# Attention and feed-forward on one core: three groups of tiles that TensorE reads, moved to other places modulo 512 bytes

## The chip, the core and the metric

The kernel runs on one core of one Trainium2 chip. The metric is the device time of one execution in microseconds; the time before is the median of three runs, 1213.74 us (1213.39 to 1214.49).

## What is computed

A layer norm feeds two branches, full attention with 32 heads of 16 and a feed-forward network with squared ReLU; their product, with a SiLU on the second, is added to the input. Cut to what matters:

```python
x = A_x                                   # 1 x 2048 x 512
xn = layernorm(x)
q, k, v = split_heads(xn @ A_wqkv)        # 32 heads of 16
p = softmax(q @ k.T * 16 ** -0.5)         # 32 x 2048 x 2048
s = merge_heads(p @ v) @ A_wo
h = relu(xn @ B_w1 + B_b1) ** 2           # 512 -> 1792
g = silu(h @ B_w2 + B_b2)                 # 1792 -> 512
return x + s * g
```

## The kernel before

Everything is float32. Matrix products other than that of the values are made in the faster float32r form from two parts of each operand, a high and a low one (h and l in the names of tiles), as high x high + high x low + low x high.

The kernel first normalizes and transposes the input and makes queries, keys and values with full-width matmuls (L127 in `linear`, L314 in `product`), and stores them in DRAM. Then the main loop goes over 64 turns of 8 steps. A step is four heads, 512 queries and 128 keys. In a turn TensorE does three things:

- Scores (L503): for each step four matmuls of 64 rows, weights 128 columns of the key tile KA, moving 512 columns of the query tile QA. Two of them, one in rows 0 to 63 and one in rows 64 to 127 of the array, run side by side. ScalarE takes the exponential of most (L507); some go through VectorE first (L526).
- Linear layers (L551, in `Block.issue`): the feed-forward network, later the output projection, in pieces between the scores, again two matmuls side by side in the two halves of the rows. First layer: weights wf1, moving the transposed input xh and xl. Second layer: weights the hidden values hh and hl, moving wf2. Output projection: weights the normalized attention output in reused tiles, moving wo in xh and xl.
- Values (L850): 8 steps of four matmuls of 32 columns each, weights slices of V (row kb of 83 numbers, 17 further for each head), moving the exponentials in P0 to P15. The profile lists each as two.

The order in a turn is written out as a string, such as `SLLSBLLLSLL0SL1LSLL/SBLLSLL0SL1LSLL0L1SLS`: S is two score matmuls, L one linear matmul in each half of the rows, 0, 1 and B are scores that go through VectorE, and / is the swap, at which the two halves change their bank and TensorE waits for a note by GpSimd (L577). VectorE and GpSimd split weights and hidden values into parts (L116, L120). SyncE loads QA, KA, V, weights and, a few turns ahead, the next xh and xl.

All tiles of SBUF are opened once at the start, by a table of names and sizes in `fast_path` (L103 to L110). Their order in it sets their addresses: a tile of n numbers takes 4n bytes of each partition, rounded up to 32, right behind the one before. P0 begins at a multiple of 512 bytes. Tiles of 1024 or 2048 numbers keep what is behind them at the same place modulo 512; a V tile of 16 x 83 = 1328 numbers takes 5312 bytes, 192 more than a multiple of 512; and each of the small tiles (st, rs, mv, okm, warm, ones, seen) takes 32 or 64. Matmuls address pieces of their tiles at distances that are multiples of 512 bytes, but for the values' slices of V.

Of the kernel before, what the change touches and what calls it, by code (L numbers as in the profile page):

```python
# [38 lines left out]
NK = S // 128  # L39
VW = 560  # L40
QW = 83
# [6 lines left out]
@with_exitstack  # L48
def mha_ffn_kernel(ctx: ExitStack, tc: tile.TileContext, x, wqkv, wo, bx, w1, b1, w2, b2, out):
    nc = tc.nc  # L50
    x, out = x[0], out[0]
    ctx.enter_context(tc.manual_schedule())
    keep = ctx.enter_context(tc.tile_pool(name="keep", bufs=1))
    dram = ctx.enter_context(tc.tile_pool(name="dram", bufs=1, space=DRAM))

    nvalid = keep.tile([1, 1], I32, name="nvalid")
    stat = keep.tile([128, 80], FT, name="stat")
    eps = keep.tile([128, 1], FT, name="eps")
    ident = keep.tile([128, 128], FT, name="ident")
    make_identity(nc, ident)  # L60

    kdram = [[dram.tile([128, 2, 1024], FT, name=f"kd{g}_{h}") for h in range(2)] for g in range(4)]
    qdram = [[dram.tile([128, 2, 512], FT, name=f"qd{g}_{c}") for c in range(NC)] for g in range(4)]
    vdram = dram.tile([NK, 128, VW], FT, name="vd")
    xdram = [dram.tile([128, 2, 4, 512], FT, name=f"xd{c}") for c in range(3)]
    sdram = {(a, p): dram.tile([128, 2, 4, 2, 128], FT, name=f"sd{a}{p}") for a in "kq" for p in range(2)}

    udram = [[dram.tile([2, 2, 16, 4, 512], FT, name=f"ud{g}_{c}") for c in range(NC)] for g in range(4)]
    zdram = [[dram.tile([4, 512], FT, name=f"zd{q}_{c}") for c in range(NC)] for q in range(NQ)]
    gdram = dram.tile([S, D], FT, name="gd")  # L70

    with tc.tile_pool(name="sb", bufs=1) as sb, ExitStack() as banks:
        fast_path(tc, sb, banks, locals())
    general_path(tc, dram, nvalid, ident, vdram, kdram, qdram, gdram, x, wo, out)


def fast_path(tc, sb, banks, env):
# [14 lines left out]
    def t(shape, dt, tag):  # L92

        cnt[0] += 1
        if tag in BUFS:
            turn[tag] = turn.get(tag, -1) + 1
            n = turn[tag] % BUFS[tag]
            p, tag = ps.get(tag), f"{tag}{places[n] if tag == 'S' else n}"
        else:
            p = None  # L100
        return (p or ps.get(tag, sb)).tile(shape, dt, tag=tag, name=f"{tag}_{cnt[0]}")

    split_tiles = [f"{a}{n}" for a in ("xh", "xl", "wf2h", "wf2l", "hh", "hl") for n in range(2)]  # L103
    for tags, n in (((f"P{i}" for i in range(16)), 1024), (("KA0", "KA1", "KA2"), 2048),
                    (("QA0", "QA1", "wf1h0", "wf1l0", *split_tiles), 1024),
                    (("T0", "T1", "wr0", "wr1", "gl", "u0", "u1", "y0", "y1"), 1024), (("ou0", "ou1", "b2b"), 512),
                    (("note",), 128), (("V0",), NK * QW), (("st0", "st1"), 12), (("rs0", "rs1", "mv0", "mv1"), 8),
                    (("okm", "warm"), 1), (("V1",), NK * QW)):
        for tag in tags:
            sb.tile([128, n], FT, tag=tag, name=f"{tag}_first")  # L110

# [451 lines left out]
    note, notes = t([1, 128], FT, "note"), [0]  # L563
# [264 lines left out]
    tags = (("P2", "gl", "P1"), ("P3", "P6", "P7"), ("wf2h0", "wf2l0", "wf2h1"), ("wf2l1", "gl", "KA2"))  # L828
# [196 lines left out]
    for j, c in enumerate(ORDER):  # L1025
        for i in range(2):
            n = per * (j + 1) + i - 1 if j < 3 else LAST + 2 + i
# [68 lines left out]
    seen = t([1, 16], FT, "seen")  # L1096
# [16 lines left out]
    for n in range(TURNS):  # L1113
        i = 8 * n
# [68 lines left out]
    ok, okm, ones = t([128, 80], FT, "ok"), t([128, 1], FT, "okm"), t([128, 1], FT, "ones")  # L1183
# [162 lines left out]
```

## Time and profile before

| | |
|---|---|
| Median of the runs | 1213.74 us |
| The profiled execution | 1212.94 us, of which the span from the first to the last instruction is 1211.2 |
| TensorE busy | 1200.1 us (99%) |
| ScalarE, VectorE, GpSimd busy | 1040.8 (86%), 845.4 (70%), 350.1 (29%) |
| Share of the DMA engines' time by the queue that SyncE feeds | 37.3% |
| Granted TensorE clock | 0.998 |

Lines of the profile name an engine, a source line, an operation and the tiles it writes and reads (`S<-QA,KA` reads QA and KA, and writes a bank S). PE is the matmul, PEld the weight load that goes ahead of it. Matmuls overlap, so a matmul's own duration is longer than its share of the time: the pace is read from the starts of one and the next. The chain of work that ended last says what each microsecond of the span was spent on.

### The profile page before, as it was taken

Reading aid. Unit: us, or ns where it says so; the run is one execution under the profiler, and the core shown is the slowest. Engines: PE = TensorE matmul, PEld = TensorE weight load, DVE = VectorE, ACT = ScalarE, POOL = GpSimd, SP = SyncE. Lnnn points to the kernel's source line nnn. Section 1 sums busy time; section 2 is a strip of 40 time slices with the busy share of each in tenths; the row PEclk is TensorE's granted clock in tenths of the full one; section 3 lists DMA queues with packets and bytes.
Section 4 is the critical chain, followed back from the end, with each engine's and each line's share of the span. In section 5 each row is a group of like instructions: output and inputs, shape, how many; then the busy total and the mean of one; then the engine's idle time right before and its main releaser. Section 6 shows DMA issues by size and latency. Waiting matters only on the chain.

```text
span 1211.2 us, 24228 instructions
## 1 busy us (share of the span) xinstructions
PE 1200.1 (99%) x9877; PEld 709.9 (59%) x9877; DVE 845.4 (70%) x1365; ACT 1040.8 (86%) x1231; POOL 350.1 (29%) x268
## 2 busy tenths in 40 slices
PE   9999999999999999999999999999999999999996
PEld 7888655555565555555555565555555555555553
DVE  7666767575866776757687676677775758777776
ACT  6655689889989889988999988889898889999993
POOL 5756523040312321304032122221230404222222
PEclk9999999999999999999999999999999999999999
DMA  7799914131343222224423133151422233464444
GB/s 290 293 371 322 332 58 137 45 111 44 97 154 109 75 69 85 67 75 149 120 77 111 46 97 85 45 183 42 118 80 80 80 99 79 132 207 151 157 140 103
DMA packets 107576, 154.91 MB, mean 128 GB/s; under 512 B 43386, under 2 KB 57736, under 8 KB 107460
## 3 DMA queue, kind: packets, MB, share of 16 engines
q1 hardware_dynamic: 104804, 144.93, 37.3%
q0 software_dynamic: 2368, 7.87, 2.2%
q8 instruction: 78, 1.28, 0.4%
q10 hardware_dynamic: 288, 0.52, 0.1%
q14 instruction: 38, 0.31, 0.1%
HBM read 103.61 MB, written 49.67 MB: 127 GB/s over the span
## 4 chain that ended last, share of the span: by engine, by line
PE 97%; DVE 1%; DMA 1%; SPq 0%; issue 0%; ACT 0%; DVEq 0%
PE acc L850 36%; PE S L551 28%; PE S L503 14%; PE B L314 5%; PE acc L503 5%; PE B L127 4%; PE lin L503 2%; PE D L314 1%; PE D L252 1%; DMA hl<-gd 0%; PE S L993 0%; PE lin L314 0%; SPq L880 0%; PE acc L314 0%; DMA P<-in_A_x_dram 0%
## 5 line engine op out<-in xcount | busy, mean ns | idle before, releaser
L507 ACT ACTIVATE P<-S 128x1024 f32<-128x1024 f32 x702 | 661.9, 1040 | 93.7 <-PE S L503 91.9
L850 PE MATMUL acc<-P,V 128*32 128x512 f32 x4096 | 453.6, 594 | 0.0
L526 DVE COPY P<-acc 128x512 f32<-128x512 f32 x322 | 222.8, 692 | 139.7 <-PE lin L503 69.2
L507 ACT ACTIVATE P<-P 128x1024 f32<-128x1024 f32 x322 | 315.0, 1090 | 0.0
L850 PEld LDWEIGHTS acc<-P,V 128*32 128x32 f32 x4096 | 126.3, 110 | 285.6 <-issue 265.6
L503 PE MATMUL S<-QA,KA 64*128 64x512 f32 x1404 | 292.0, 405 | 0.0
L526 DVE COPY P<-lin 128x512 f32<-128x512 f32 x322 | 220.6, 685 | 1.5 <-PE lin L503 0.6
L503 PEld LDWEIGHTS S<-QA,KA 64*128 64x128 f32 x1404 | 134.6, 184 | 111.2 <-issue 41.8
L503 PE MATMUL lin<-QA,KA 64*128 64x512 f32 x322 | 126.8, 394 | 0.0
L503 PE MATMUL acc<-QA,KA 64*128 64x512 f32 x322 | 126.6, 393 | 0.1
L120 POOL TENSOR_TENSOR wf1l<-wr,wf1h 128x1024 fp32r<-128x1024 f32 x28 | 68.4, 2442 | 176.9 <-DVE wf1h L116 108.4
L577 POOL MEMSET note<- 1x1 f32 x68 | 6.0, 88 | 383.2 <-PE S L551 381.7
L551 PE MATMUL S<-xl,wf1h 64*128 64x512 f32 x464 | 95.8, 389 | 0.0
L120 POOL TENSOR_TENSOR hl<-T,hh 128x1024 fp32r<-128x1024 f32 x28 | 79.9, 2855 | 52.9 <-DVE hh L116 52.9
L120 POOL TENSOR_TENSOR wf2l<-wr,wf2h 128x1024 fp32r<-128x1024 f32 x28 | 67.2, 2401 | 90.5 <-DVE wf2h L116 90.5
L551 PE MATMUL S<-xh,wf1l 64*128 64x512 f32 x480 | 91.3, 388 | 0.0
L551 PE MATMUL S<-wf2l,hh 64*128 64x512 f32 x448 | 90.3, 390 | 0.0
L876 DVE TENSOR_TENSOR ou<-acc,ou 128x512 f32<-128x512 f32 x31 | 21.4, 692 | 96.8 <-PE acc L850 91.0
L551 PE MATMUL S<-wf2h,hl 64*128 64x512 f32 x448 | 82.9, 388 | 0.0
L551 PE MATMUL S<-xh,wf1h 64*128 64x512 f32 x480 | 77.7, 392 | 0.0
L551 PE MATMUL S<-wf2h,hh 64*128 64x512 f32 x448 | 71.7, 393 | 0.0
L503 PEld LDWEIGHTS acc<-QA,KA 64*128 64x128 f32 x322 | 59.3, 184 | 17.1 <-DVE P L526 2.4
(370 smaller groups left out, 1427.7 us busy)
## 6 DMA issues: line engine op xcount, KB each, us to landing
wr<-in_B_w_dram SPq DMA_DIRECT2D x56, 512.0 KB
QA<-qd SPq DMA_DIRECT2D x128, 128.0 KB
KA<-kd SPq DMA_DIRECT2D x64, 256.0 KB
u<-ud SPq DMA_DIRECT2D x15, 512.0 KB
kd<-P SPq DMA_DIRECT2D x11, 512.0 KB
V<-vd SPq DMA_DIRECT2D x8, 664.0 KB
qd<-P SPq DMA_DIRECT2D x9, 512.0 KB
vd<-P SPq DMA_DIRECT2D x16, 280.0 KB
```

The lines of the kernel that those rows point to most:

```text
L120: leng.tensor_tensor(lo, src, hi.bitcast(FT), op=OP.subtract)
L127: mm(dst, lhs(a, k), rhs(b, k), start=n == 0, stop=n == len(todo) - 1)
L252: nc.tensor.transpose(halves[k // 2][:, k % 2, 128 * j:128 * j + 128], xnorm[c, i][:, j, 128 * k:128 * k + 128], ident)
L314: mm(dst, left[a][:, k], right[b][:, k], start=n == 0, stop=n == 5)
L503: mm(dst, k[r, p, 128 * (kb % 8):128 * (kb % 8) + 128], q[r, p], start=True, stop=True)
L507: act.activation(ptile[i, p], src, AF.Exp, scale=SCALE)
L526: dve.tensor_copy(ptile[i, p][:, hp], sides[hp])
L551: ins = mm(bank, self.lhs(a, k)[r], self.rhs(b, k)[r], start=n == 0 and self.at[other] == 0, stop=n == len(self.todo[half]) - 1 and self.a ...
L577: f = pool.memset(note[:, notes[0]:notes[0] + 1], 0.0)
L850: mm(sides[0][32 * j:32 * j + 32], vq[qd][:, kb, 17 * j:17 * j + 32], ptile[i, j // 2][:, j % 2], start=first, stop=last)
L876: dve.tensor_tensor(ou, sides[0], part[0], op=OP.add)
```

## The change

The table that opens the tiles is put in another order. Every engine has the same instructions in the same order with the same waits; addresses alone differ.

```diff
-    split_tiles = [f"{a}{n}" for a in ("xh", "xl", "wf2h", "wf2l", "hh", "hl") for n in range(2)]
-    for tags, n in (((f"P{i}" for i in range(16)), 1024), (("KA0", "KA1", "KA2"), 2048),
-                    (("QA0", "QA1", "wf1h0", "wf1l0", *split_tiles), 1024),
+    second = [f"{a}{n}" for a in ("wf2h", "wf2l", "hh", "hl") for n in range(2)]
+    for tags, n in (((f"P{i}" for i in range(16)), 1024), (("QA0", "QA1", "wf1h0", "wf1l0"), 1024),
                     (("T0", "T1", "wr0", "wr1", "gl", "u0", "u1", "y0", "y1"), 1024), (("ou0", "ou1", "b2b"), 512),
-                    (("note",), 128), (("V0",), NK * QW), (("st0", "st1"), 12), (("rs0", "rs1", "mv0", "mv1"), 8),
-                    (("okm", "warm"), 1), (("V1",), NK * QW)):
+                    (("note",), 128), (("st0",), 12), (("xh0", "xh1", "xl0", "xl1"), 1024), (("st1",), 12),
+                    (("rs0", "rs1", "mv0"), 8), (("okm",), 1), (("KA0", "KA1", "KA2"), 2048), (("mv1", "warm", "ones"), 8),
+                    (("seen",), 16), (second, 1024), (("V0", "V1"), NK * QW)):
         for tag in tags:
             sb.tile([128, n], FT, tag=tag, name=f"{tag}_first")
```

The places that follow, in bytes modulo 512:

| Tiles | before | after |
|---|---|---|
| P0 to P15, QA, wf1, T, wr, gl, u, y, ou, b2b | 0 | 0 |
| xh, xl | 0 | 64 |
| KA0 to KA2 | 0 | 256 |
| wf2h, wf2l, hh, hl | 0 | 416 |
| V0, V1 | 0, 0 | 416, 96 |

## The prediction

> **What bounds the kernel now.** I read the busy times first, then the chain of work that ended last, then the rows of TensorE by line.
>
> ```profile
> span 1211.2 us, 24228 instructions
> PE 1200.1 (99%) x9877; PEld 709.9 (59%) x9877; DVE 845.4 (70%) x1365; ACT 1040.8 (86%) x1231; POOL 350.1 (29%) x268
> PE 97%; DVE 1%; DMA 1%; SPq 0%; issue 0%; ACT 0%; DVEq 0%
> PE acc L850 36%; PE S L551 28%; PE S L503 14%; PE B L314 5%; PE acc L503 5%; PE B L127 4%; PE lin L503 2%; PE D L314 1%; PE D L252 1%; DMA hl<-gd 0%; PE S L993 0%; PE lin L314 0%; SPq L880 0%; PE acc L314 0%; DMA P<-in_A_x_dram 0%
> ```
>
> TensorE is 97% of the chain, so a change counts if it alters the pace of the matmuls or makes them wait. The change adds, removes and reorders no instruction and no wait; it only gives tiles other addresses. So the question is whether the pace of a matmul, or of something that TensorE waits for, depends on where its operands stand.
>
> The chain has three kinds of matmul. Values (L850, 36%) run four at a time in column strips. Scores (L503) and linear layers (L551) run two at a time, one in each half of the rows; I call such a couple a slot. The preparation (L127, L314) runs one full-width matmul after another. The first pair of rows below is the count of the row-half matmuls (L551, then L503, from the view by windows), the next three are steps of the chain.
>
> ```profile
> 0.00:1211.20 1211.20, 506.45 (x3036) 1.00 0.40 128
> 0.00:1211.20 1211.20, 441.23 (x2048) 1.00 0.40 128
> 97.87 10.88 PE B L127 x48
> 21.01 7.18 PE B L314 x30
> 213.58 7.00 PE acc L850 x64
> ```
>
> (3036 + 2048) / 2 = 2542 slots. The steady pace of the full-width matmuls is 10.88 / 48 = 0.2267 us; just behind waits it is 7.18 / 30 = 0.239. The values go 16 quartets in 7.00, 0.4375 each.
>
> Now one turn of the main loop, in the timeline of TensorE (start, length, what, count):
>
> ```profile
> 600.30 0.63 PE L551 MATMUL S<-xh,wf1h 64*128 64x512 f32 x4
> 600.76 0.41 PE L503 MATMUL S<-QA,KA 64*128 64x512 f32 x2
> ...
> 602.84 0.39 PE L503 MATMUL S<-QA,KA 64*128 64x512 f32 x2
> 603.07 0.39 PE L551 MATMUL S<-xh,wf1l 64*128 64x512 f32 x1
> ...
> 603.98 0.62 PE L551 MATMUL S<-xh,wf1l 64*128 64x512 f32 x4
> 604.43 0.44 PE L503 MATMUL S<-QA,KA 64*128 64x512 f32 x2
> ...
> 604.94 0.64 PE L551 MATMUL S<-xh,wf1h 64*128 64x512 f32 x4
> 605.40 0.41 PE L503 MATMUL S<-QA,KA 64*128 64x512 f32 x2
> ...
> 608.86 0.43 PE L551 MATMUL S<-xh,wf1l 64*128 64x512 f32 x2
> 609.09 0.44 PE L503 MATMUL S<-QA,KA 64*128 64x512 f32 x2
> ```
>
> From 600.30 to 602.84 there are 11 slots: 0.2309 each. From 602.84 to 603.98 there are 5: 0.228. After the swap at 604.4 there are 18 from 604.94 to 609.09: 0.2306. In all 34 slots in 2.54 + 1.14 + 4.15 = 7.83, or 0.2303 each. So a slot costs 3.6 ns more than the steady pace, most of it in the stretch behind each wait. Over 2542 slots that is 9.2 us, the part of the pace that is visibly not fixed.
>
> **The change part by part.** *Places.* Tiles are laid end to end, each rounded up to 32 bytes in a partition. Before, every operand of every slot starts at 0 modulo 512: all strides are 512 bytes or a multiple. Afterwards xh and xl stand at 64, KA at 256, the eight tiles of the second layer (wf2, hh, hl) at 416; QA, wf1 and P stay at 0. V0 and V1, 0 before, go to 416 and 96. So of the 5082 weight loads that follow another matmul in their row half, 3706 (73%, counted over the program's order and addresses) now read at a place other than that of the stream that is running; the rest are second-layer slots behind one another (416 under 416) and wf1 under QA (0 under 0).
>
> *Values.* The weights of L850 are slices of V at 332 kb + 68 j bytes, so before the change they already stand at many places modulo 512.
>
> ```profile
> L850 PEld LDWEIGHTS acc<-P,V x4096: 105/110/111, 147.0 to 1193.1; 128*32 128x32 f32 x196
> L850 PE MATMUL acc<-P,V x4096: 592/592/618, 147.0 to 1193.5; 128*32 128x512 f32 x196
> ```
>
> Minimum, median and maximum nearly agree over 4096 of each, so moving V costs nothing: 0.
>
> *Scores and linear layers.* No row shows these at another place. Their durations spread more than those of the values:
>
> ```profile
> L503 PEld LDWEIGHTS S<-QA,KA x1404: 182/184/187, 133.6 to 1184.3; 64*128 64x128 f32 x176
> L503 PE MATMUL S<-QA,KA x1404: 383/392/502, 133.6 to 1184.5; 64*128 64x512 f32 x176
> ```
>
> The bounds: (a) the places do not matter: 0. (b) What is not steady comes from streams and weight loads that meet at one place, and goes where the places now differ: 73% of 9.2 = 6.7 us less. (c) The steady pace holds such a cost too. Half a quartet of the values takes 0.4375 / 2 = 0.219 with weights spread over many places; if slots fell to that, it would be 0.2303 - 0.219 = 11.3 ns on 73% of 2542, 21 us less. That halving a quartet gives the bare stream is an assumption. (d) On the other side, differing places disturb the steady pace: below, 5 us more; at worst the 12 ns between 0.2267 and 0.239 on 73% of the slots, 22 us more. Nearest to the rows is (b), since the 3.6 ns are measured in the slots themselves. I take 6.7 us.
>
> *Transfers and other engines.* Loads into KA, xh, xl and V, and the work of GpSimd and VectorE on hh, hl and wf2, meet new addresses. Their cost is put at nothing, because TensorE hardly waits for them. These are its weight loads' longest waits, and the GpSimd step with the least room in the loop, with the first matmul block that certainly needs its result:
>
> ```profile
> PEld acc L850 <- issue: 265.6, 889, 0.3
> PEld S L503 <- issue: 41.8, 51, 0.8
> PEld S L503 <- ACT P L507: 22.7, 105, 0.8
> PEld acc L850 <- DVE P L526: 18.8, 63, 0.4
> PEld S L503 <- ACT seen L1101: 8.4, 10, 0.8
> PEld S L551 <- DVE y L643: 3.4, 4, 0.8
> ...
> 664.88 2.38 POOL L120 TENSOR_TENSOR hl<-T,hh 128x1024 fp32r<-128x1024 f32 x1 [1.89 <-DVE hh L116]
> ...
> 670.59 0.62 PE L551 MATMUL S<-wf2h,hl 64*128 64x512 f32 x4
> ```
>
> The "issue" waits lie under running matmuls, since PE is 99% busy; no transfer and no split is among the rest. The split of hl ends at 667.26 and is used by 670.59: it may take 2.3 times as long (3.3 us more) before anything waits. If that cover is gone, each of 28 splits of hl that took 1 us beyond it costs 28 us; no row speaks for that.
>
> **Sum.** The profiled execution took 1212.94 us (span 1211.2 and 1.7 around it). Less 6.7 that is 1206.2; against the median of the runs, 1213.74, it is 1207.0, which I forecast.
>
> **The rivals.**
>
> *Place does not matter.* Against (b) speaks that the slow pace also appears where one full-width stream runs alone behind a wait (0.239 above, then 0.2267), which looks like a start-up of the engine and no meeting of streams; and the values' rows show no dependence on the place of weights. Then 0 changes: 1213.7. For it speaks too a page: the Trainium skill, "SBUF — State Buffer", section "Who interferes with whom", gives TensorE two independent read ports, one for the moving operand and one for weight loads, and says that PE never waits on anyone; by it the gain is 0 and the time stays 1213.7. The values' rows agree with it; no row tests it for moving operands away from 0. That the change does not do what it says (that the period that matters is not 512 bytes) ends at the same time. Chance 0.20.
>
> *Mixed places keep the pace unsteady.* Now that all operands stand at one place, one slot is like the next, and after some 11 slots the pace settles at 0.2267 to 0.228. With KA, QA, xh and wf2 at four places the order of a turn (S L L S ...) changes the distance at nearly every slot. If settling needs equal distances, the early pace stays: the 5 settled slots of the half turn above, and their like, go to 0.2309 or more. Taking for the 73% of slots that differ the middle between 0.2267 and 0.239, 0.2329, gives 2.6 ns x 1856 = 4.8 us more: 1218.5. It decides as soon as the pace late in a half turn lies above 0.2303. Speaking for it: full-width runs, with equal places and no interleaving, settle best. Against: nothing shows that settling depends on addresses. Chance 0.26, and 0.05 more for a worse loss, towards (d), 1236.
>
> *The steady pace falls too*, (c): 1213.7 - 21 = 1193. Speaking for it is only the values' faster stream. Chance 0.06.
>
> **How the numbers follow.** Forecast (b): chance 0.43, with its own range of 1200 to 1211. The chances: faster by over 0.2% (2.4 us, about what a measurement of this kernel can tell from no change) 0.43 + 0.06 = 0.49; within it 0.20; slower 0.26 + 0.05 = 0.31. The range of 8 in 10 reaches over (b), the unchanged time and the unsteady pace, from 1199 to 1219, and leaves out the full (c) and the worst of (d).
>
> **What would show it.** Right: in the profile afterwards the slots from the start of a half turn take below 0.230 and the chain's shares of L551 and L503 fall, by some 7 us together, while L127, L314 and L850 keep their pace. In the rows of L503 the median of 392 ns would come nearer to the minimum of 383. Wrong: equal paces (place does not matter), or 0.232 and more late in a half turn (unsteady). A wait of weight loads for POOL hl, or for a transfer into KA or xh, that is now absent would show that the cover I assumed is gone. It would also be wrong if the pace of L850 changed, since the values' many places are my only evidence on places.

## The result, and the profile after

The changed kernel takes 1219.53 us (median of four runs, 1219.04 to 1220.32) against 1213.57 us (four runs, 1212.11 to 1214.49) in the same comparison: 6.0 us slower, a ratio of 1.005 with an interval of 1.0037 to 1.0062. I had forecast 1207.0, and the time lies just above the upper end of the range, 1219.

The page shows where. TensorE is busy 5.5 us longer (1205.6 against 1200.1), ScalarE 3.1, the others at most 0.5, and the span is 6.0 us longer:

```profile
span 1217.2 us, 24228 instructions
PE 1205.6 (99%) x9877; PEld 712.8 (59%) x9877; DVE 845.9 (69%) x1365; ACT 1043.9 (86%) x1231; POOL 350.2 (29%) x268
```

The values run as before. The rows of L850 (minimum, median, maximum of one; first and last start) also divide the loss:

```profile
L850 PEld LDWEIGHTS acc<-P,V x4096: 106/110/111, 148.4 to 1198.8; 128*32 128x32 f32 x196
L850 PE MATMUL acc<-P,V x4096: 592/592/618, 148.4 to 1199.2; 128*32 128x512 f32 x196
```

The first starts at 148.4 in place of 147.0, so the preparation lost 1.4 us (its first matmul of L127 starts at 8.1 in both); from the first to the last it takes 1050.4 in place of 1046.1, so the main loop lost 4.3; behind it 0.3 is left.

In the preparation three stretches of the chain of 48 matmuls each (start, length) are alike but for the place of one operand. Before and after:

```profile
34.09 11.01 PE B L127 x48
60.47 10.93 PE B L127 x48
```

```profile
34.16 11.20 PE B L127 x48
60.86 10.91 PE B L127 x48
98.66 11.20 PE B L127 x48
```

The moving operand is at 0 in all. The weights are the transposed input: xh and xl in the first and third, now at 64, and KA in the second, now at 256. At 64 the third goes from 10.88 (the row shown in the prediction) to 11.20, 0.2333 a matmul in place of 0.2267. At 256 the second stays as it was.

In the main loop the same turn as before (timeline of TensorE):

```profile
603.43 0.63 PE L551 MATMUL S<-xh,wf1h 64*128 64x512 f32 x4
603.89 0.39 PE L503 MATMUL S<-QA,KA 64*128 64x512 f32 x2
...
607.60 0.44 PE L503 MATMUL S<-QA,KA 64*128 64x512 f32 x2
...
608.08 0.67 PE L551 MATMUL S<-xh,wf1h 64*128 64x512 f32 x4
...
612.28 0.40 PE L503 MATMUL S<-QA,KA 64*128 64x512 f32 x2
```

18 slots take 4.17 from 603.43 to 607.60 (0.2317 each; before, 600.30 to 604.43, 4.13) and 18 take 4.20 from 608.08 to 612.28 (0.2333 each; before 4.15). Now all slots of the trace: the steps from the first start of one slot to that of the next, those of 0.215 to 0.250 us alone (2306 before, 2314 after), parted into the first ten behind a longer step and those that follow:

| | first ten, ns | later ones, ns |
|---|---|---|
| before | 231.5 | 228.3 |
| after | 232.3 | 232.7 |

Other ways of telling the two halves apart move these figures by up to 0.5 ns. The slots behind a wait take 0.8 ns more; what is lost is above all the settling to a faster pace that came after them.

### The profile page after: what moved, and what is told of

Its sections match the earlier page's. It is cut to its first block, busy times and chain, and to the rows that moved or that the text cites. A ratio compares the mean times of both kernels' runs of the same rounds, so it can differ in the third digit from the quotient of the medians.

```text
span 1217.2 us, 24228 instructions
## 1 busy us (share of the span) xinstructions
PE 1205.6 (99%) x9877; PEld 712.8 (59%) x9877; DVE 845.9 (69%) x1365; ACT 1043.9 (86%) x1231; POOL 350.2 (29%) x268
## 4 chain that ended last, share of the span: by engine, by line
PE 97%; DVE 1%; DMA 1%; SPq 0%; issue 0%; ACT 0%; DVEq 0%
PE acc L850 36%; PE S L551 28%; PE S L503 14%; PE B L314 5%; PE acc L503 5%; PE B L127 4%; PE lin L503 2%; PE D L314 1%; PE D L252 1%; DMA hl<-gd 0%; PE S L993 0%; SPq L880 0%; PE lin L314 0%; PE acc L314 0%; DMA P<-in_A_x_dram 0%
## 5 line engine op out<-in xcount | busy, mean ns | idle before, releaser
L850 PE MATMUL acc<-P,V 128*32 128x512 f32 x4096 | 453.5, 594 | 0.0
L850 PEld LDWEIGHTS acc<-P,V 128*32 128x32 f32 x4096 | 126.1, 110 | 287.9 <-issue 265.3
L120 POOL TENSOR_TENSOR hl<-T,hh 128x1024 fp32r<-128x1024 f32 x28 | 80.0, 2859 | 52.9 <-DVE hh L116 52.9
```

What stands on the lines that cost most here:

```text
L120: leng.tensor_tensor(lo, src, hi.bitcast(FT), op=OP.subtract)
L850: mm(sides[0][32 * j:32 * j + 32], vq[qd][:, kb, 17 * j:17 * j + 32], ptile[i, j // 2][:, j % 2], start=first, stop=last)
```

## The experiments

All kernels of the table of tiles are the kernel before with another order of the table alone; "all else at 0" is modulo 512, and small tiles (st, rs, mv, okm, warm, zc) fill up to the next place. The diffs show the lines that set the places and leave out the rest of the table; xs_tiles are xh and xl, ks_tiles KA, second_tiles wf2, hh and hl, weight_tiles wf1, hh and hl. Their ratios are to runs of the kernel before on the same chip, and the differences in us are between medians. The kernels of bare streams ran once each.

**Bare streams.** A kernel of its own; its core is

```diff
+    for k in range(16):
+        b = bank("w" + "abcdefghijklmnop"[k])
+        for _ in range(COUNT):
+            one(b, 32 * k, 0)            # place of the weights, place of the moving operand
...
+            one(b, p, p)                 # both
+            one(b, 0, p)                 # mov
+            one(b, p if i % 2 else 0, 0) # alt
```

> This kernel leaves the reference's work out: it only runs streams of 40 full-width matmuls (128 weights, 512 moving columns, float32r) one behind another, with the weights 0, 32, ... 480 bytes past the place of the moving operand (banks wa to wp), then both operands moved together (both), the moving one alone (mov), weights alternating between two places (alt), and couples in the two halves of the rows (half, sides, turn). Distance theory: at distance 0 the pace settles at 0.2267 us, at other distances it stays near 0.231 to 0.234; both operands moved together keep 0.2267. Own-place theory (an operand off 0 is slower to read whatever stands beside it): the streams with both moved are slow as well, about 0.232. No-place theory (what moved the time is which region of the memory a tile stands in): 0.2267 in every one of them.

Its timeline; each stream has 40 matmuls, so the step from one start to the next, divided by 40, is the pace. wa is distance 0, wb 32, wc 64, wf 160, wg 192, wi 256, wk 320:

```profile
21.66 9.24 PE L36 MATMUL wa<-m,w 128*128 128x512 f32 x40
30.73 9.49 PE L36 MATMUL wb<-m,w 128*128 128x512 f32 x40
40.06 9.50 PE L36 MATMUL wc<-m,w 128*128 128x512 f32 x40
49.39 9.52 PE L36 MATMUL wd<-m,w 128*128 128x512 f32 x40
...
68.04 9.50 PE L36 MATMUL wf<-m,w 128*128 128x512 f32 x40
77.38 9.33 PE L36 MATMUL wg<-m,w 128*128 128x512 f32 x40
86.55 9.49 PE L36 MATMUL wh<-m,w 128*128 128x512 f32 x40
95.87 9.24 PE L36 MATMUL wi<-m,w 128*128 128x512 f32 x40
104.95 9.49 PE L36 MATMUL wj<-m,w 128*128 128x512 f32 x40
114.27 9.50 PE L36 MATMUL wk<-m,w 128*128 128x512 f32 x40
...
179.19 9.26 PE L36 MATMUL bothb<-m,w 128*128 128x512 f32 x40
188.29 9.28 PE L36 MATMUL bothc<-m,w 128*128 128x512 f32 x40
...
206.52 9.50 PE L36 MATMUL mova<-m,w 128*128 128x512 f32 x40
215.85 9.33 PE L36 MATMUL movb<-m,w 128*128 128x512 f32 x40
```

Distance 0 gives 9.07 / 40 = 0.2268 and 256 gives 9.08 / 40 = 0.2270. 32 and 64 give 0.2333, 96 gives 0.234, 192 gives 0.2293 (9.17 / 40). The lengths repeat from wi on as from wa: the period is 256 bytes, not 512. With both operands moved to 64 (bothb) the pace is that of 0 (9.10 / 40 = 0.2275, with its settling), and with the moving operand alone at 32 (mova) it is slow again. The moving operand at 64 (movb) runs as weights at 192 do (0.2293). So the distance decides and not an operand's own place: no operand is slower by itself, and no distance is faster than 0.

The last streams of this kernel, by the steps between their starts: weights that alternate between 0 and 64 take 0.230, between 0 and 160 0.232, between 0 and 256 0.2267. Couples in the two halves settle at 0.2267 at distances 0 and 256, and stay at 0.2334 at 64 and 160. With one half wholly at 0 and the other wholly at 64 (sides) both settle. Couples that alternate between weights at 256 over a stream at 0 and weights at 0 over a stream at 64, as the turns of the changed kernel do (turn), take 0.231.

**The order without the places.** The groups in the order of the changed kernel, every one of them at 0:

```diff
+                    (("note",), 128),
+                    (xs_tiles, 1024),
+                    (ks_tiles, 2048),
+                    (second_tiles, 1024),
+                    (("V0",), NK * QW),
```

> The tiles in the order of the changed kernel, but with the small tiles so spread that every group stands at 0 modulo 512 again. Distance theory and own-place theory: the time of before, 1213.6 us within 1 us. Region theory: the time of the changed kernel, 1219.5 us.

1213.54 us, ratio 1.0000 (0.9991 to 1.0009). It is the place modulo the period that counts, not the region of the memory.

**One group at a time.** xh and xl alone at 64:

```diff
+                    (("st0",), 12),
+                    (xs_tiles, 1024),
+                    (("zc0",), 64), (("st1",), 12), (("rs0",), 8), (("rs1",), 8), (("mv0",), 8), (("mv1",), 8),
```

> Only xh and xl at 64, all else at 0. Distance theory: a third of the weight loads (those under a stream from xh or xl) then differ from the running stream, 1692 of 5082, against 3706 with the whole change, which cost 6.0 us; so 2.7 us more than before, 1216.3 us. Own-place theory: 1692 of some 5080 moving operands are off 0, 6.0 us times their share among the operands moved by the whole change (1692 of 6680 operand uses): 1.5 us more, 1215.1. Region theory: no forecast, but the order matters and not the 64.

1216.93 us, ratio 1.0029 (1.0019 to 1.0038), 3.5 us more (2.3 to 4.6). The second layer alone at 416:

```diff
+                    (("zc0",), 64), (("st0",), 12), (("rs0",), 8), (("rs1",), 8), (("mv0",), 8),
+                    (second_tiles, 1024),
+                    (("mv1",), 8), (("okm",), 1), (("warm",), 1),
```

> Only wf2, hh and hl at 416, all else at 0. Distance theory: loads of hidden values under queries and loads of keys under wf2 differ, about 1560 of 5082, plus some 250 in the output projection: 6.0 us times 1810 / 3706, 2.9 us more than before, 1216.5. The second-layer slots behind one another keep distance 0. Own-place theory: both operands of 1344 second-layer matmuls are off 0, 2.6 us more, 1216.2, with the loss in the slots of L551 behind one another.

1217.29 us, ratio 1.0031 (1.0020 to 1.0042), 3.8 us more. The forecast of the distance theory lies within the measured interval in both (counted over the trace, 1556 loads differ and not 1810, which gives 2.5, at the interval's lower end); that of the own-place theory lies outside it for xh and xl, and inside it for the second layer. There the trace tells more: from a score to a second-layer slot the step rose from 231.0 to 234.5 ns, back from 230.0 to 232.9, from one second-layer slot to the next, both at 416, from 230.4 to 232.2. So the loss is largest where the place changes, but not only there.

The keys alone, at 256 and at 128:

```diff
+                    (("zc0",), 64),
+                    (ks_tiles, 2048),
+                    (("zc1",), 64),
```

```diff
+                    (("st0",), 12), (("st1",), 12),
+                    (ks_tiles, 2048),
+                    (("zc0",), 64), (("rs0",), 8), (("rs1",), 8), (("mv0",), 8), (("mv1",), 8),
```

> Only KA at 256, all else at 0. Distance theory with the period of 256 bytes that the bare streams showed (0.2267 at 0 and at 256): no loss, 1213.5 us within 1 us. The same theory with a period of 512: 2048 of 5082 loads differ (those of keys and those under queries make more), 3.3 us more, 1216.8. Own-place theory: weights of 2048 matmuls off 0, 1.8 us more, 1215.3.

> Only KA at 128, all else at 0: the same 2048 weight loads as with 256, now at a distance that the bare streams showed at 0.2324. Distance theory: 3.5 us from xh and xl at 64 for 1692 loads give 2.07 ns a load, so 4.2 us more here, 1217.7. Own-place theory: as with 256, 1215.3.

At 256: 1213.87 us, ratio 1.0003 (0.9994 to 1.0012), no loss. At 128: 1217.30 us, ratio 1.0032 (1.0019 to 1.0044), 4.0 us more. The same 2048 weight loads, the same order of tiles: the period of 256 holds in the kernel, the own-place theory (1.8 us at both) misses both intervals, and of the change's three groups the keys are the one that cost nothing.

V0 and V1 alone at 416 and 96:

```diff
+                    (("zc0",), 64), (("st0",), 12), (("rs0",), 8), (("rs1",), 8), (("mv0",), 8),
+                    (("V0",), NK * QW),
+                    (("V1",), NK * QW)):
```

> Only V0 and V1 at 416 and 96, all else at 0. My step on the values, under all theories: no change, 1213.5 us within 1 us. A rival: the loads of V or the preparation, where V0 and V1 hold sums that are multiplied full-width, cost up to 1 us.

1214.19 us, ratio 1.0005 (0.9996 to 1.0014): no loss that can be measured; the rival's 1 us in the preparation lies inside the interval and is not excluded.

The single losses, 3.5 + 3.8 + 0.6 + 0.9, come to more than the 6.0 of the whole; their intervals are some 1 us to each side, so whether they add up is not settled.

**Back to distance 0 within the changed kernel.** xh and xl at 0, the second layer at 256:

```diff
+                    (xs_tiles, 1024),
+                    (("zc0",), 64),
+                    (ks_tiles, 2048),
+                    (second_tiles, 1024),
+                    (("st0",), 12), (("rs0",), 8), (("rs1",), 8), (("mv0",), 8),
+                    (("V0",), NK * QW),
+                    (("V1",), NK * QW)):
```

> The changed kernel with xh and xl back at 0 and the second layer at 256 in place of 416; KA stays at 256, V0 and V1 at 416 and 96, and the order of tiles is the changed one. Distance theory with a period of 256: every distance is 0 again, so 1213.5 us within 1 us although most groups stand off 0. Own-place theory: weights and moving operands of the scores and the second layer are off 0, some 4 us more, 1217.5.

1214.06 us, ratio 1.0003 (0.9994 to 1.0012). Two corrections of places take back all of the loss that can be measured. All of these places are 0 modulo 256, so in the kernel this does not tell distance 0 from a place of 0 modulo 256; the streams bothb and bothc, with both operands at 64 or at 160, do.

**Streams that restart.** The bare streams again, in row halves, 20 slots behind a wait each:

```diff
+    for k in range(16):
+        pairs("step" + "abcdefghijklmnop"[k], [[(16 * k, 0), (16 * k, 0)]])
```

> This kernel leaves the reference's work out: streams of 20 slots (couples in the two halves of the rows), each behind a wait as the half turns of the kernel are, with the weights 0, 16, ... 240 bytes past the moving operand (stepa to stepp), some finer distances (fine), and one half at 0 with the other at 0, 64, 128, 192 (side). Distance theory: after the wait the pace falls to 0.2267 within some 11 slots at distance 0 alone (a mean of 0.230 over 20 slots), and stays at 0.229 to 0.234 elsewhere. Rival, start-up theory (the slow slots behind a wait are a start-up of the engine that nothing about addresses changes): the first 10 slots take the same at every distance, some 0.232. A distance whose 20 slots take less than those at 0 would be a better layout.

The lengths of distance 0, 16, 32, 96, 192 and 240, and of a second stream at 0 (sidea):

```profile
21.45 4.85 PE L36 MATMUL stepa<-m,w 64*128 64x512 f32 x40
26.36 4.93 PE L36 MATMUL stepb<-m,w 64*128 64x512 f32 x40
31.35 4.96 PE L36 MATMUL stepc<-m,w 64*128 64x512 f32 x40
...
51.24 4.98 PE L36 MATMUL stepg<-m,w 64*128 64x512 f32 x40
...
81.07 4.89 PE L36 MATMUL stepm<-m,w 64*128 64x512 f32 x40
...
95.93 4.88 PE L36 MATMUL stepp<-m,w 64*128 64x512 f32 x40
...
130.66 4.86 PE L36 MATMUL sidea<-m,w 64*128 64x512 f32 x40
```

Single starts of stepa in one row half lie 335, 235, 233, 236, 224, 231, 236, 228, 232, 231, 227, 227, 226 ns apart and then stay; behind the first, those of stepc stay between 229 and 235, those of stepg between 231 and 238. The first interval is alike at every distance (333 to 343 ns in the sixteen steps), and the first ten take 2.39 to 2.44 us in all. The nine behind the first average 231.8 in stepa, 229.0 in sidea, which settled after 6 slots, 234.3 at 96 and 228.0 at 240. So a slow start is there at distance 0 too, and it differs from one stream to the next; that it is the same at every distance, as the start-up theory has it, is not shown. Settling to 0.2267 exists at distance 0, and at 16 in one row half (the other went on at 0.2333). No distance took its 20 slots in less than the faster stream at 0: from first start to last 4.437 for sidea and 4.461 for stepa, against 4.450 at 240.

**Nearly all weights at one distance.** The weights of KA, wf1, hh and hl at 96, every moving operand at 0, and the same at 192 (192 of the 5084 row-half matmuls, in the output projection, have their weights in wf2, at 0):

```diff
+                    (("st0",), 12), (("rs0",), 8),
+                    (ks_tiles, 2048),
+                    (weight_tiles, 1024),
+                    (("zc0",), 64), (("st1",), 12), (("rs1",), 8), (("mv0",), 8), (("mv1",), 8),
```

```diff
+                    (("st0",), 12), (("st1",), 12), (("rs0",), 8), (("rs1",), 8),
+                    (ks_tiles, 2048),
+                    (weight_tiles, 1024),
+                    (("zc0",), 64), (("mv0",), 8), (("mv1",), 8),
```

> All weights of the main loop (KA, wf1, hh, hl) at 96, all moving operands (QA, xh, xl, wf2) at 0, the worst distance of the restarted streams: 20 slots took 4.548 us there against 4.461 at distance 0. Distance theory: 0.087 us more in each of 128 half turns of about 20 slots, 11 us, so 1224.6 us. Own-place theory: weights alone off 0, the same loss as with the weights at 192 beside it, some 3 us, 1216.5.

> The same tiles as with 96, the weights at 192: 20 slots took 4.468 us there, since the pace is 0.229 at once and does not fall further. Distance theory: 0.007 us more in each of 128 half turns, 0.9 us, so 1214.4 us, the same as before within what can be measured. Own-place theory: the same as at 96, 1216.5.

At 96: 1220.09 us, ratio 1.0053 (1.0039 to 1.0067), 6.8 us more in place of 11. At 192: 1216.08 us, ratio 1.0021 (1.0011 to 1.0030), 2.8 more in place of 0.9. The order of the two is as the distance theory has it, and they lie apart, against the own-place theory. Both sizes were off. The profiled executions, 1216.98 and 1220.87 us, were the longest of each, so they are set against the profile of before, 1212.94. At 192 the first value starts at 149.3 in place of 147.0: 2.3 of 4.0 us lie in the preparation, whose mixed distances I had not priced, and the main loop takes 1.2 more, near the forecast 0.9. Not all of the 2.3 need come from places: the first matmul of L127 already starts 1.1 later (9.2 in place of 8.1), and with V alone moved, where no loss was measured, the first value started at 148.4.

At 96, 2.7 of 7.9 us lie in the preparation and 5.0 in the main loop, less than half of the 11. The pace of the slots, counted as in the table, rose by 3.4 ns, over the 2440 steps from slot to slot in the main loop 8.3 us. A part was taken back in the steps of more than 250 ns, those behind waits: what they hold beyond 230 ns each came to 10.6 us in place of 13.6. The longest listed waits shifted as follows (line numbers of this kernel are higher by 8 than those of the kernel before):

```profile
PEld acc L858 <- DVE P L534: 21.9, 65, 0.4
PEld S L511 <- ACT P L515: 13.3, 57, 0.8
PEld S L559 <- POOL note L585: 10.1, 57, 0.2
```

Before they were 18.8 in 63, 22.7 in 105 and 2.0 in 13 places. What is put to ScalarE fell by 9.4 us and what is put to GpSimd and VectorE rose by 11.2, so the rows show who came last, and not whose slack paid.

**Which distance.** Streams in which two kinds of matmul alternate, shorter weight loads, and plain float32:

```diff
+    stream("own", [(0, 0), (64, 64)])
+    stream("cross", [(0, 64), (64, 0)])
...
+    for cols, c in ((32, "short"), (64, "middle"), (96, "long")):
+        for k, p in enumerate((0, 64, 160)):
+            stream(c + "abc"[k], [(p, 0)], cols)
```

> This kernel leaves the reference's work out: full-width streams of 40 float32r matmuls in which two kinds of matmul alternate. In 'own' the weights stand where their own moving operand stands (both 0, then both 64), so each weight load meets a running stream 64 away; in 'cross' the weights stand 64 from their own moving operand, but each load meets a running stream at its own place (ownb and crossb: 160 in place of 64). Distance to the running stream: plain and cross 0.2267, own 0.231 to 0.234. Distance to the own moving operand: plain and own 0.2267, cross 0.231 to 0.234. Then weights of 32, 64 and 96 columns at distance 0, 64 and 160 (short, middle, long), and plain float32 matmuls (full). Meeting theory (the load of the next weights and the running stream read at the same time and the loss grows with what the load reads): at 32 columns a loss below 2 ns in place of 6.7 at distance 64. Rival, start theory (the loss comes from the first address alone): the same 6.7 ns at every width. Plain float32, which takes four times as long per pass of its columns as the values' rows suggest, shows no dependence under both, within 3 ns.

```profile
22.19 9.23 PE L45 MATMUL plain<-m,w 128*128 128x512 f32 x40
31.26 9.42 PE L45 MATMUL own<-m,w 128*128 128x512 f32 x40
40.52 9.49 PE L45 MATMUL cross<-m,w 128*128 128x512 f32 x40
49.85 9.24 PE L45 MATMUL plainb<-m,w 128*128 128x512 f32 x40
58.92 9.53 PE L45 MATMUL ownb<-m,w 128*128 128x512 f32 x40
68.29 9.36 PE L45 MATMUL crossb<-m,w 128*128 128x512 f32 x40
77.49 9.43 PE L45 MATMUL shorta<-m,w 128*32 128x512 f32 x40
86.76 9.42 PE L45 MATMUL shortb<-m,w 128*32 128x512 f32 x40
...
133.09 9.37 PE L45 MATMUL longa<-m,w 128*96 128x512 f32 x40
142.29 9.30 PE L45 MATMUL longb<-m,w 128*96 128x512 f32 x40
151.43 9.41 PE L45 MATMUL longc<-m,w 128*96 128x512 f32 x40
160.68 34.50 PE L59 MATMUL fulla<-raw 128*128 128x512 f32 x80
195.01 34.50 PE L59 MATMUL fullb<-raw 128*128 128x512 f32 x80
```

Both forecasts on the alternating streams failed: own takes 0.2315 and cross 0.2333 with 64, and 0.2343 and 0.2300 with 160. So neither the running stream nor the own moving operand decides alone, and which of the two is slower depends on the distance; here the settled pace came only where weights and streams all stood at one place modulo 256. The forecasts for single groups of tiles rested on the count of loads away from the running stream, which is thus not the whole measure, though those for one group lay within the intervals.

The theories on the width are not settled. Weights of 32 columns read a quarter as much, and distance 64 cost them nothing against distance 0, as the meeting theory has it; but their stream is slow even at distance 0 (shorta, 9.27 / 40 = 0.2317), which neither theory forecast. With 96 columns distance 64 is even the faster one (longb, 9.14 / 40 = 0.2285, against longa, 0.2300). The settled pace was seen with weights of 128 columns alone. Plain float32 takes 34.33 / 40 = 0.858 a matmul at distances 0, 64 and 160.

## Why the prediction was wrong

*What bounds the kernel* held. TensorE's pace carries the loss, in the slots and, for 1.4 us, in the full-width matmuls of the preparation; no transfer and no split comes into its waits. The wait for GpSimd's note at the swap, 2.0 us in 13 places before, is listed with 9.7 in 56, but the four slots up to the first behind the swap take 0.95 (607.13 to 608.08) against 0.96 before (603.98 to 604.94), so at this swap that is a label and not a loss.

*Values at no cost* was right as far as it can be measured: their rows are the same, and moving V alone showed no loss beyond the noise.

*Step (b) failed*, in its sign: "what is not steady comes from streams and weight loads that meet at one place, and goes where the places now differ". I had measured the excess (9.2 us, behind each wait) and then given it a cause that no row showed. The restarts show that a slow start is there at distance 0 and that no distance takes it away with a gain over 20 slots, and the bare streams that the steady pace of 0.2267 needs distance 0. In the kernel the early slots went from 231.5 to 232.3 ns and the later ones from 228.3 to 232.7, in place of falling. What I took for the fault was the condition for settling. The evidence lay in the prediction itself, in the rival's line that full-width runs with equal places settle best.

*Bound (c)*, that the steady pace holds such a cost too, is wrong at the distances measured: no distance in steps of 32 was below 0.2267. Plain float32 has the same pace at the three distances tried, so the values' rows, which I took as evidence on places, say nothing on float32r.

*The rival of mixed places* was right, in its mechanism and its sign, and low in the total. It said 4.8 us, for the slots alone; the main loop lost 4.3, and 6.0 were measured, since the preparation, 1.4 us, was missing from it. Its point of decision, a late pace above 0.2303, is met by 0.2327. That 4.8 came so near the loop's 4.3 is in part luck, as errors both ways met. Of the loads 73% was too many, as a distance of 256 counts as 0: with that period the same count gives 3121 of 5082, 61%. The later slots rose by 4.4 ns, more than the 2.6 taken. And not all of it arrived: the mean over the slots of the table rose from 230.1 to 232.5 ns, 5.9 us over the 2440 steps in the main loop, while the steps of more than 250 ns, those behind waits, hold 12.3 us beyond 230 ns each in place of 13.6 (13.3, 13.2 and 14.2 in three kernels without a loss: the order alone, KA at 256, and back to 0). Whose waits these were, the rows do not say: what is put to ScalarE fell by 6.6 us, and what is put to GpSimd's note rose by 7.7.

```profile
PEld S L503 <- ACT P L507: 16.1, 74, 0.8
PEld S L551 <- POOL note L577: 9.7, 56, 0.2
```

*Place does not matter* fell with the single groups. The page named there, the Trainium skill, "SBUF — State Buffer", section "Who interferes with whom", lets PE wait on no one for its reads; the bare streams, with nothing else running, differ by 0.2333 against 0.2267 by address alone. That does not show another engine in the way, but a gain or loss of 0 does not follow from the rule.

*Transfers and other engines at nothing* held: the splits of hl took 2859 ns in place of 2855. (The room that I gave the split shown, 3.3 us beyond its 2.38, is 2.4 times its time and not 2.3.)

What stays open is what in the engine settles. The runs saw the settled pace only with loads of 128 columns and with the weights and moving operands of a row half at one place modulo 256, but for the one row half with weights 16 bytes off; a lock between two periodic reads would look so, but that is argued and not shown. Two layouts were not tried in the kernel: weights 16 bytes off, and all operands at one common place other than 0 modulo 256, which the bare streams show to settle.

## What to carry to other kernels

For dense float32r matmuls on TensorE with weights of 128 columns, put weights and moving operands at one place modulo 256 bytes; here that was worth 6 us of 1213, and shifting groups apart to avoid conflicts was the loss. A slow start behind a wait is in itself no sign of conflicts: compare it with a bare stream before giving it a cause. And a slower pace can cost less than its sum: here the steps behind waits gave some 1.3 us back.

## What the runs showed of the hardware

Not expected: the pace of identical matmuls depends on the distance of their operands with a period of 256 bytes, from 0.2267 at 0 to 0.234 at 96, with 0.229 at 192; behind a wait a stream at distance 0 settles at 0.2267 only after 6 to 11 slots; streams that alternate between two places, 64 or 160 apart, stay at 0.2315 and 0.2343 even where each pair of operands stands together; and with weights of 32 or 96 columns the stream did not settle to 0.2267 at all (0.2317 and 0.2300 at distance 0). Plain float32 matmuls, at 0.858, show none of this.
